# A gated attention and MLP kernel: which x chunks are turned by TensorE, and the order of the first transfers on SP's queue

## The chip, the cores and the metric

The kernel runs on one core of a Trainium2 chip. The metric is device time in microseconds (us) of one execution; of several executions the median counts, and less is better. Besides, one execution is taken by the hardware profiler; all durations of single instructions come from that one.

## What is computed

The input x has 2048 rows (tokens) of 640 bf16 numbers. Two blocks read it, and a gate per row mixes them:

```
g = sigmoid((x * gate_w).sum(-1))
out = g * A(x) + (1 - g) * B(x)

A: q, k, v = split(x @ wqkv)                 # 32 heads of 20
   phi(t) = where(t > 0, t + 1, exp(t)) + 1e-6
   kv = sum_s phi(k) v ;  z = sum_s phi(k)
   o  = phi(q) kv / (phi(q) z + 1e-6) ;  A = o @ wo
B: h  = gelu(layernorm(x) @ w1), its four quarters shifted by 1, -1, 2, -2 rows
   x1 = x + h @ w2 ;  B = x1 + gelu(layernorm(x1) @ w3) @ w4
```

For the change only the start of A matters: k = x @ wk, where wk is the middle third of wqkv, and phi(k).

## The kernel before

TensorE (PE) contracts over the 128 partitions, so x @ wk needs x transposed. The rows are tiled into 16 chunks of 128 (NCH), the 640 columns into 5 slabs of 128 (DC). `x_sb` holds x as it lies in memory, `xT` holds it transposed, `wkg` holds wk in five slabs with two more columns (the gate's weights and ones), hence 642 columns.

`k_mm(c, p, dc)` (L258) adds slab dc of chunk c into PSUM buffer p with two matmuls, of 512 and 130 columns. When a chunk has its five slabs, `k_post` (L263) applies phi: an exponential on ScalarE (ACT, L252), then two operations on VectorE (DVE, L255 and L256), the second of which writes phi(k) to `pk`; then it releases the PSUM buffer. There are four such buffers, handed out by `alloc` and `release` in the order of a list, `free`. From chunk 5 on, `g_unit(0, c)` is woven in: two matmuls of `x_sb` chunk c with `pk` chunk c (L269), which accumulate x^T phi(k) and hold one more PSUM buffer.

The order of the instructions on each engine is written by hand (`manual_schedule`). DMAs are issued from two queues: SP's (`sp`) and ACT's (`aq`). A queue issues in the order of the program and stands still while the next DMA waits for a semaphore. In the head it goes like this:

- ACT's queue: the gate's weights (L162), then slabs 0, 1 and 2 of wk (L166, `load_wk`). SP's queue: x chunks 0, 1 and 2 into `x_sb` (L156, `load_x`), then slabs 3 and 4 of wk in one DMA (L173).
- PE runs warm-up matmuls (L317) on zeros, then turns chunk 0 by five transposes against the identity matrix into PSUM (`x_tr`, L326), which DVE and ACT copy to `xT` (`x_cp`, L330 and L331). Then a small transpose of the gate's weights (L336), another warm-up, and chunk 1 the same way.
- A memset of DVE (L342) writes one element of `xT` in the place of chunk 3. The first transposing DMA (`load_xT`, L159), of chunk 3, overwrites that element and so waits for the memset. Behind it on SP stand all the other DMAs of `late_loads` (L285): transposing DMAs of the chunks up to 15, the x chunks from 3 on in between, then wq (L301), w1, wv, wo and w2. POOL's copies (L312) are part of it too.
- PE does slab 0 of chunks 0 and 1, turns chunk 2, and finishes the slabs of the three chunks in a woven order. Chunks 3 to 15 follow in a loop, chunk by chunk, then the q stage (L404), which reads wq.

After that follow the q stage, the layernorm and w1 stage, w2, w3 and w4, each a long run of matmuls; the change does not touch them.

Of the kernel before, what the change touches and what calls it, by code (L numbers as in the profile page):

```python
# [16 lines left out]
def kernel(  # L17
# [13 lines left out]
    nc = tc.nc  # L31
    P = 128
# [3 lines left out]
    NCH = S // P  # L36
# [28 lines left out]
    xT = RXT[:].rearrange("p (j s) -> p j s", j=DC)  # L65
# [71 lines left out]
    free = [0, 1, 2, 3]  # L137

    def alloc():
        return free.pop(0)  # L140
# [11 lines left out]
    sp, aq = nc.sync, nc.scalar  # L152
    xv = x2.rearrange("(c p) d -> p c d", p=P)

    def load_x(c0, c1):
        sp.dma_start(x_sb[:, c0:c1, :], xv[:, c0:c1, :])  # L156

    def load_xT(c0, c1):
        sp.dma_start_transpose(xT[:, :, c0 * P:c1 * P], x2[c0 * P:c1 * P, :])  # L159
# [5 lines left out]
    def load_wk(q, dc):  # L165
        q.dma_start(wkg[:, dc, 0:D], A_wqkv[dc * P:(dc + 1) * P, D:2 * D])  # L166

    for dc in range(3):
        load_wk(aq, dc)
    load_x(0, 1)  # L170
    load_x(1, 2)
    load_x(2, 3)
    sp.dma_start(wkg[:, 3:5, 0:D], A_wqkv[3 * P:5 * P, D:2 * D].rearrange("(j p) d -> p j d", p=P))  # L173


# [65 lines left out]
    def pop(q, n=1):  # L241
        for _ in range(n):
            if q:
                q.pop(0)()
# [13 lines left out]
    def k_mm(c, p, dc):  # L258
        for (n0, n1) in ((0, 512), (512, KW)):
            mm(PP[p][:, n0:n1], lhsT=xT[:, dc, c * P:(c + 1) * P], rhs=wkg[:, dc, n0:n1],  # L260
               start=(dc == 0), stop=(dc == DC - 1))

    def k_post(c, p):  # L263
        phi(pk[:, c, :], PP[p][:, 0:D], D, (ym[:, c, :], PP[p][:, D:D + 2]))
        release(p)
# [12 lines left out]
    def g_unit(i, c):  # L278
        if c == 0:
            gp[0] = alloc()  # L280
        g_step(i, c, gp[0])
        if c == NCH - 1:
            g_post(i, gp[0])

    def late_loads():  # L285
        load_xT(3, 4)
        load_xT(4, 5)
        load_xT(5, 6)
        load_xT(6, 7)
        load_x(3, 4)  # L290
        load_xT(7, 8)
        load_x(4, 6)
        load_xT(8, 10)
        load_x(6, 9)
        load_xT(10, 11)
        load_xT(11, 13)
        load_x(9, 12)
        load_xT(13, 16)
        load_x(12, 16)
        rows = lambda w, a, b: w[:, a:b].rearrange("(j p) d -> p j d", p=P)  # L300
        sp.dma_start(wq, rows(A_wqkv, 0, D))  # L301
        sp.dma_start(w1, rows(B_w1, 0, D))
        sp.dma_start(wv, rows(A_wqkv, 2 * D, 3 * D))
        sp.dma_start(wo6[0:GW, 0:5, :], A_wo[0:5 * GW, :].rearrange("(g r) d -> r g d", r=GW))
        sp.dma_start(wo6[0:GW, 5, :], A_wo[G5:D, :])
        sp.dma_start(w2[:, 0:4, :], B_w2.rearrange("(g c) d -> c g d", c=CG)[0:P])
        for g in range(4):
            sp.dma_start(w2[32 * g:32 * (g + 1), 4, :], B_w2[CG * g + P:CG * (g + 1), :])
        w1g = w1.rearrange("p k (g c) -> p k g c", c=CG)
        w1x4 = w1x.rearrange("p k (g c) -> p k g c", g=4)  # L310
        for g in range(4):
            nc.gpsimd.tensor_copy(w1x4[:, :, g, :], w1g[:, :, g, P:CG])  # L312


    def warm_up(n):
        for _ in range(n):
            mm(PP[1][:, 512:1024], lhsT=warm[:, 0:1].to_broadcast([P, P]), rhs=warm[:, 0:1].to_broadcast([P, 512]),  # L317
               start=True, stop=True)

    warm_up(5)  # L320

    def x_tr(c, a, b):
        ta, tb = PP[a][:, 0:512].bitcast(BF16), PP[b][:, 0:512].bitcast(BF16)
        for dc in range(DC):
            t, k = (ta, dc) if dc < 3 else (tb, dc - 3)
            nc.tensor.transpose(t[:, k * P:(k + 1) * P], x_sb[:, c, dc * P:(dc + 1) * P], ident[:])  # L326

    def x_cp(c, a, b):
        ta, tb = PP[a][:, 0:512].bitcast(BF16), PP[b][:, 0:512].bitcast(BF16)
        nc.vector.tensor_copy(xT[:, 0:3, c * P:(c + 1) * P], ta[:, 0:3 * P].rearrange("p (j s) -> p j s", j=3))  # L330
        act(xT[:, 3:5, c * P:(c + 1) * P], tb[:, 0:2 * P].rearrange("p (j s) -> p j s", j=2), ACT.Copy)  # L331
# [3 lines left out]
    tg = PP[0][:, 512:1024].bitcast(BF16)  # L335
    nc.tensor.transpose(tg[:, 0:DC], g5[0:DC, :], ident[0:DC, 0:DC])  # L336
    warm_up(1)
    for dc in range(DC):
        nc.vector.tensor_copy(wkg[:, dc, D:D + 1], tg[:, dc:dc + 1])
    x_tr(1, 1, 0)  # L340
    x_cp(1, 1, 0)
    nc.vector.memset(xT[:, 0, 3 * P:3 * P + 1], 0.0)  # L342
    late_loads()
    hp = (3, 2, 1)
    del free[1:]
    k_mm(0, 3, 0)
    k_mm(1, 2, 0)
    x_tr(2, 1, 0)
    x_cp(2, 1, 0)
    k_mm(0, 3, 1)  # L350
    k_mm(1, 2, 1)
    k_mm(2, 1, 0)
    k_mm(2, 1, 1)
    for c in range(3):
        k_mm(c, hp[c], 2)
    for c in range(3):
        for dc in (3, 4):
            k_mm(c, hp[c], dc)
        k_post(c, hp[c])


    for c in range(3, NCH):
        p = alloc()
        for dc in range(DC):
            k_mm(c, p, dc)
        k_post(c, p)
        for k in {5: (0, 1), 6: (2, 3), 7: (4,)}.get(c, (c - 3,) if c > 5 else ()):
            g_unit(0, k)
        if c % 2 == 0:
            pop(ln1_s)  # L370


# [359 lines left out]
```

## Time and profile before

| what | us |
|---|---|
| median of 5 runs | 265.08 (264.41 to 265.44) |
| the profiled execution's own time | 264.86 |
| its span in the profile | 263.1 |
| PE busy | 257.4 |
| DVE, ACT, POOL busy | 126.6, 109.7, 36.3 |
| five transposes of one chunk on PE (L326), in the chain | 0.53 |
| issue of one transposing DMA on SP (L159), chunks 3 to 7 | 1.22 to 1.29 |
| first transposing DMA issued at | 5.36 |
| first matmul of the k stage at | 4.91 |
| first matmul of the q stage at | 31.7 |

How to read it: times count from the start of the span. PE is the matmul side of TensorE, PEld its weight loads, which overlap with the matmuls. L12 is line 12 of the kernel. A group's line names the engine, the operation, the tile that it writes and those that it reads, the shapes and the count. In the timeline the first number is the start, the second the length. A bracket or "<-" behind an idle time names what ended it. SPq and ACTq are the parts of SP and ACT that issue DMAs; "to landing" is from the issue of a DMA to its last semaphore update. Tiles appear by the names of their memory: RXT is `xT`, RXH holds `x_sb`, RA holds `wkg` and `wq`, RPK is `pk`, and pp is PSUM.

### The profile page before, as it was taken

How to read it: one execution, taken by the hardware profiler on the slowest of the kernel's cores; microseconds unless marked ns; L12 is line 12 of the kernel's file. 1: busy time of each engine (PE TensorE's matmuls, PEld its weight loads, DVE VectorE, ACT ScalarE, POOL GpSimd, SP SyncE). 2: the span in 40 equal slices, each digit the busy share in tenths (PEclk: the TensorE clock that was granted, in tenths of full speed). 3: DMA queues.
4: the chain of work that ended last, by engine and by line, in shares of the span. 5: the costliest groups of instructions: out<-in, count | busy, mean ns of one | idle time of the engine just before them, and what ended most of it. 6: DMA issues, size and time to landing. Idle time of an engine off the chain costs nothing.

```text
span 263.1 us, 4153 instructions
## 1 busy us (share of the span) xinstructions
PE 257.4 (98%) x1634; PEld 136.3 (52%) x1666; DVE 126.6 (48%) x227; ACT 109.7 (42%) x163; POOL 36.3 (14%) x120
## 2 busy tenths in 40 slices
PE   8999999999999999999999999999999999999995
PEld 4555555555564545554444455555544445555552
DVE  1487658988995257999920023422310002334133
ACT  3466654554454761335977432202034445202200
POOL 7000053030200001446870000000000000000000
PEclk9999999999999999999999999999999999999999
DMA  6699998442242059992542000200200000010011
GB/s 200 131 214 211 351 268 177 93 52 50 50 52 50 13 139 404 325 164 50 108 96 50 0 2 0 75 27 0 77 25 0 0 2 0 0 51 26 25 52 50
DMA packets 42372, 24.07 MB, mean 91 GB/s; under 512 B 31137, under 2 KB 41585, under 8 KB 42353
## 3 DMA queue, kind: packets, MB, share of 16 engines
q1 hardware_dynamic: 41767, 23.28, 36.9%
q10 hardware_dynamic: 586, 0.53, 0.6%
q8 instruction: 13, 0.21, 0.4%
q14 instruction: 6, 0.05, 0.0%
HBM read 12.98 MB, written 3.44 MB: 62 GB/s over the span
## 4 chain that ended last, share of the span: by engine, by line
PE 98%; issue 1%; DVE 0%
PE pp L643 21%; PE pp L587 20%; PE pp L260 9%; PE pp L617 8%; PE pp L269 8%; PE pp L404 8%; PE pp L437 8%; PE pp L572 8%; PE pp L596 2%; PE pp L317 1%; PE pp L649 1%; PE pp L606 1%; PE pp L326 1%; PE pp L457 1%; PE pp L469 1%
## 5 line engine op out<-in xcount | busy, mean ns | idle before, releaser
L643 PE MATMUL pp<-RB,RXH 128*128 128x128 bf16 (+1 forms) x407 | 57.7, 297 | 0.7 <-issue 0.3
L587 PE MATMUL pp<-lnxT,RA 128*128 128x512 bf16 x236 | 51.9, 379 | 0.2
L643 PEld LDWEIGHTS <-RXH 128*128 128x128 bf16 x416 | 31.8, 98 | 24.5
L587 PEld LDWEIGHTS <-RA 128*128 128x128 bf16 x240 | 23.4, 98 | 28.1
L589 ACT ACTIVATE RXH<-pp 128x1024 bf16<-128x1024 f32 x24 | 24.3, 1021 | 30.5 <-PE pp L587 30.5
L252 ACT ACTIVATE eb<-pp 128x640 bf16<-128x640 f32 (+1 forms) x26 | 21.4, 829 | 25.2 <-PE pp L404 16.3
L620 ACT ACTIVATE RXH<-pp,g_all 128x640 f32<-128x640 f32 x16 | 12.7, 794 | 45.4 <-PE pp L617 45.4
L622 DVE SCALAR_TENSOR_TENSOR RPK<-RPK,omg,RXH 128x640 f32<-128x640 f32 x8 | 7.1, 884 | 41.5 <-ACT RXH L620 41.5
L269 PE MATMUL pp<-RPK,RXH 128*128 128x512 bf16 (+1 forms) x158 | 25.1, 298 | 0.1
L260 PE MATMUL pp<-RA,RXT 128*128 128x130 bf16 (+1 forms) x156 | 24.3, 303 | 0.2
L404 PE MATMUL pp<-RXT,RA 128*128 128x512 bf16 x98 | 23.1, 379 | 0.1
L617 PE MATMUL pp<-Mp,pqT 128*128 128x128 bf16 (+1 forms) x158 | 22.9, 298 | 0.1
L622 DVE SCALAR_TENSOR_TENSOR RXT<-RXT,omg,RXH 128x640 f32<-128x640 f32 x8 | 7.1, 884 | 31.9 <-ACT RXH L620 31.9
L572 PE MATMUL pp<-w,RXH 128*128 128x128 bf16 (+1 forms) x157 | 21.7, 297 | 0.2
L437 PE MATMUL pp<-lnxT,RB 128*128 128x512 bf16 x76 | 18.1, 379 | 0.2
L269 PEld LDWEIGHTS <-RXH 128*128 128x128 bf16 x160 | 12.7, 98 | 10.4
L260 PEld LDWEIGHTS <-RXT 128*128 128x128 bf16 x160 | 12.7, 100 | 9.6 <-DVE RXT L342 0.3
L617 PEld LDWEIGHTS <-pqT 128*128 128x128 bf16 x160 | 12.3, 98 | 9.9 <-issue 0.4
L572 PEld LDWEIGHTS <-RXH 128*128 128x128 bf16 x160 | 12.3, 98 | 9.5
L404 PEld LDWEIGHTS <-RA 128*128 128x128 bf16 x100 | 11.1, 117 | 9.2 <-DMA RA<-in_A_wqkv_dram 0.3
L255 DVE TENSOR_SCALAR eb<-eb 128x640 bf16<-128x640 bf16 (+1 forms) x26 | 9.5, 364 | 11.7 <-ACT eb L252 11.7
L256 DVE SCALAR_TENSOR_TENSOR RPK<-pp,eb 128x640 bf16<-128x640 f32 x16 | 13.2, 824 | 2.1
(112 smaller groups left out, 238.8 us busy)
## 6 DMA issues: line engine op xcount, KB each, us to landing
out_dram<-RXH SPq DMA_DIRECT2D x15, 160.0 KB, 1.8
RA<-in_B_w_dram SPq DMA_DIRECT2D x5, 432.0 KB, 6.8
RA<-in_A_wqkv_dram SPq DMA_DIRECT2D x2, 800.0 KB, 6.7
RB<-in_B_w_dram SPq DMA_DIRECT2D x1, 1120.0 KB, 9.1
RXH<-in_A_x_dram SPq DMA_DIRECT2D x2, 480.0 KB, 4.4
RB<-in_B_w_dram SPq DMA_DIRECT2D x1, 960.0 KB, 10.4
RB<-in_B_w_dram SPq DMA_DIRECT2D x1, 800.0 KB, 8.4
Mp<-Mscr SPq DMA_DIRECT2D x1, 800.0 KB, 4.3
```

Source lines behind the costliest of these rows:

```text
L252: act(e[:, 0:n], src, ACT.Exp)
L256: nc.vector.scalar_tensor_tensor(dst, src, 0.0, e[:, 0:n], op0=ALU.max, op1=ALU.add)
L260: mm(PP[p][:, n0:n1], lhsT=xT[:, dc, c * P:(c + 1) * P], rhs=wkg[:, dc, n0:n1], start=(dc == 0), stop=(dc == DC - 1))
L269: mm(PP[p][:, n0:n1], lhsT=x_sb[:, c, i * P:(i + 1) * P], rhs=pk[:, c, n0:n1], start=(c == 0), stop=(c == NCH - 1))
L404: mm(PP[p][:, tt * 512:(tt + 1) * 512], lhsT=wqp[:, dc, j], rhs=xT[:, dc, t0:t0 + 512], start=(dc == 0), stop=(dc == DC - 1))
L437: mm(PP[p][:, tt * 512:(tt + 1) * 512], lhsT=lh, rhs=lnxT[:, dc, t0:t0 + 512], start=(dc == 0), stop=(dc == DC - 1))
L572: mm(PP[p][:, n0:n1], lhsT=hsT[:, fc, 2 + c * P:2 + (c + 1) * P], rhs=w2[:, fc, n0:n1], start=(fc == 0), stop=(fc == DC - 1))
L587: mm(PP[p][:, k * 512:(k + 1) * 512], lhsT=w3[:, dc, (fc + k) * P:(fc + k + 1) * P], rhs=lnxT[:, dc, t * 512:(t + 1) * 512], start=(dc == ...
L589: act(h2T[:, t % 2, fc:fc + 2, :], PP[p][:].rearrange("p (k s) -> p k s", k=2), ACT.Gelu_apprx_tanh)
L617: mm(PP[p][:, n0:n1], lhsT=pqT[:, j, c * P:(c + 1) * P], rhs=Mp[:, j, n0:n1], start=(j == 0), stop=(j == DC - 1))
L622: nc.vector.scalar_tensor_tensor(x1(c), x1(c), omg[:, c:c + 1], ga, op0=ALU.mult, op1=ALU.add)
L643: mm(PP[ps[m]][:, n0:n1], lhsT=h2T[:, k, fc, i * P:(i + 1) * P], rhs=w4[:, fc, n0:n1], start=(m < 2 and fc == 0), stop=(m >= 2 and fc == N ...
```

## The change

Slab 2 of wk goes from ACT's queue to SP's, to the place where x chunk 2 was loaded. Chunk 2 is no longer turned by PE: a transposing DMA brings it, the first of five (chunks 2 to 6) that open `late_loads`. The memset that held back the first of these is gone, and `late_loads` is called ahead of PE's warm-up, so that on SP it stands directly behind slabs 3 and 4. Chunk 2 in its natural layout is loaded together with chunk 3, after the five. On PE chunks 0 and 1 go through slabs 0, 1 and 2 in turn, then each through slabs 3 and 4; chunk 2 has become the first of the loop. The first four PSUM buffers are given out as before (3, 2, 1, 0).

```diff
-    for dc in range(3):
-        load_wk(aq, dc)
+    load_wk(aq, 0)
+    load_wk(aq, 1)
     load_x(0, 1)
     load_x(1, 2)
-    load_x(2, 3)
+    load_wk(sp, 2)
     sp.dma_start(wkg[:, 3:5, 0:D], A_wqkv[3 * P:5 * P, D:2 * D].rearrange("(j p) d -> p j d", p=P))
...
     def late_loads():
-        load_xT(3, 4)
-        load_xT(4, 5)
-        load_xT(5, 6)
-        load_xT(6, 7)
-        load_x(3, 4)
+        for c in range(2, 7):
+            load_xT(c, c + 1)
+        load_x(2, 4)
         load_xT(7, 8)
...
+    late_loads()
     def warm_up(n):
...
     x_tr(1, 1, 0)
     x_cp(1, 1, 0)
-    nc.vector.memset(xT[:, 0, 3 * P:3 * P + 1], 0.0)
-    late_loads()
-    hp = (3, 2, 1)
-    del free[1:]
-    k_mm(0, 3, 0)
-    k_mm(1, 2, 0)
-    x_tr(2, 1, 0)
-    x_cp(2, 1, 0)
-    k_mm(0, 3, 1)
-    k_mm(1, 2, 1)
-    k_mm(2, 1, 0)
-    k_mm(2, 1, 1)
-    for c in range(3):
-        k_mm(c, hp[c], 2)
-    for c in range(3):
+    hp = (3, 2)
+    free[:] = [1, 0]
+    for dc in range(3):
+        for c in range(2):
+            k_mm(c, hp[c], dc)
+    for c in range(2):
         for dc in (3, 4):
             k_mm(c, hp[c], dc)
         k_post(c, hp[c])
...
-    for c in range(3, NCH):
+    for c in range(2, NCH):
...
-        if c % 2 == 0:
+        if c > 3 and c % 2 == 0:
             pop(ln1_s)
```

## The prediction

> **What bounds the kernel now.** I read the page's busy shares and its chain first. TensorE (PE) is busy for 98% of the span and makes up 98% of the chain that ended last, so only time taken from PE, or PE's idle time, moves the end.
>
> ```profile
> PE 257.4 (98%) x1634; PEld 136.3 (52%) x1666; DVE 126.6 (48%) x227; ACT 109.7 (42%) x163; POOL 36.3 (14%) x120
> ...
> PE 98%; issue 1%; DVE 0%
> ```
>
> Next the chain of waits over the first 30 us, which prices PE's pieces (start, length, what).
>
> ```profile
> 5.12 1.07 PE pp L260 x4
> 6.19 0.53 PE pp L326 x5
> 6.73 3.35 PE pp L260 x24
> ...
> 18.66 1.36 PE pp L260 x10
> ```
>
> The third chunk's five transposes (L326) are 0.53 us of it. Two matmuls of a k_mm (512 and 130 columns) cost 0.535 us before them (1.07/2), but 0.272 us later (1.36/5): PE starts at half speed. Mean durations of the 128x512 form by window say the same: 632 ns in 4.8 to 6.0 us, 379 ns in 8 to 14 us. The single records put the change near 6.8 us: matmuls of 512 columns start 0.427 us apart until then, 0.215 us after. The PEclk row (9 throughout) doesn't show it.
>
> ```profile
> L260 PE MATMUL pp<-RA,RXT 128*128 128x512 bf16 x2 | 1.2, 632 | 0.0
> ...
> L260 PE MATMUL pp<-RA,RXT 128*128 128x512 bf16 x22 | 6.2, 379 | 0.0
> ```
>
> Then who waits in 6 to 33 us, and what SP's queue waits for:
>
> ```profile
> PEld L404 <- DMA RA<-in_A_wqkv_dram: 0.3, 1, 0.3
> PEld L260 <- DMA RXT<-in_A_x_dram: 0.2, 1, 0.2
> ...
> SPq L159 <- DVE RXT L342: 2.7, 1, 2.7
> ```
>
> PE hardly waits for DMA, but two transfers have no slack: the transposition of chunks 13 to 15 (landed 26.66 us, asked for at 26.6) and wq (issued at 24.92, 6.7 us to landing, 31.67; PE is free at 31.61). The SP queue stood 2.7 us behind L342's memset before it issued the first transposition at 5.36. Third, the timeline around 14.9 us:
>
> ```profile
> 14.08 0.82 DVE L256 SCALAR_TENSOR_TENSOR RPK<-pp,eb 128x640 bf16<-128x640 f32 x1
> 14.22 0.43 PEld L269 LDWEIGHTS <-RXH 128*128 128x128 bf16 x4
> 14.27 0.71 PE L269 MATMUL pp<-RPK,RXH 128*128 128x512 bf16 x4
> ...
> 14.76 1.38 PEld L260 LDWEIGHTS <-RXT 128*128 128x128 bf16 x10
> ...
> 14.96 1.52 PE L260 MATMUL pp<-RA,RXT 128*128 128x512 bf16 x10
> ```
>
> Chunk 6 takes the PSUM buffer that VectorE (DVE) frees at 14.90; its matmul starts at 14.96, 0.14 us later than its four predecessors require. I compared all PE starts after 6.86 us with their columns: real holes are only this one (0.14), chunk 13 (0.03) and wq (0.10); gaps of 0.215 us are missing records. After 32 us there are only small fixed gaps, none on a DMA. What the head saves therefore reaches the end.
>
> **The change, part by part.**
>
> *Transposes of chunk 2 removed.* By the row it is 0.53 us. [...] If speed comes at the same moment, the 0.53 us is filled with k_mm work at half speed that would have cost 0.27 at full speed: gain 0.27. Had it ended with the work, 0.53. I take 0.27, since everything before 5.99 us stays as it is; 0.53 is the upper end. The two copies (DVE 0.36, ACT 0.38 us) and L342's memset (0.06) lie beside PE and are worth nothing: the second k_mm waits for x_cp(1), done at 5.31, not for the memset.
>
> *wk slab 2 from ACT to SP, in the place of x chunk 2.* x chunk 2 landed 3.5 us after its issue at 1.72, so slab 2 lands near 5.2 instead of 6.7. ACT issues one DMA fewer (0.45 us), ahead of its table load; nothing on PE waits for that. The new k_mm order (both chunks, slab by slab) asks for slab 2 at 6.9 us and for slabs 3 and 4 at 7.45. Those landed at 6.9 before (issue 2.18, 4.7 us), and now have 160 KB less beside them: 6.4 to 6.9. No wait; 0.5 us of cover.
>
> *Transpositions directly behind the loads on SP, without the gate.* Issues take 1.31 us each from 2.65 us: chunk 2 at 2.65, chunks 3 to 6 at 3.96, 5.27, 6.58, 7.89; x chunks 2 and 3 at 9.2; chunk 7 at 9.85 instead of 11.26. What follows on SP, up to wq, goes 1.4 us earlier: 2.7 won, one more transposition paid. SP holds only DMA issues here; POOL's four copies (L312) keep their place among POOL's instructions. When does PE ask? Two k_mm done at 5.99; 0.775 us at half speed is 1.45 k_mm; the other 6.55 at 0.272 take until 8.55. Chunk 2 is asked for at 8.55, chunks 3, 4, 5 at 9.9, 11.3, 12.6; two g_units (0.27 each) later chunk 6 at 14.5.
>
> When does chunk 2 land? Lower end 3.2 us from issue, the shortest in the window: 5.9. Upper end: chunk 10 behind a 480 KB load took 6.2 us (15.07 to its semaphore at 21.27): 8.85, a wait of 0.3. The nearest row is chunks 8 and 9, directly behind a 320 KB load as here, 4.8 us: 7.45. I take 7.5, with 1.1 us of cover. Chunks 3 to 6 land about 3.3 us after their issue, as before, or 0.8 us after one another: latest 8.3, 9.1, 9.9, 11.2. All earlier than asked for. If the cover is gone, each microsecond of lateness costs one.
>
> [...]
>
> *x chunk 2 later.* Its first reader is g_unit(0, 2) at about 15.9 us. Issued at 9.2, 4.1 us (as the 320 KB x load at 12.53), it lands near 13.3. Free.
>
> *Post-processing starts earlier.* Chunk 0's k_mm end at 8.0 instead of 9.1, as it no longer waits for chunk 2's. DVE's chain (1.19 us each: 0.32 + 0.82 and gaps) frees chunk 3's buffer at 13.8 instead of 14.9, and chunk 6 asks at 14.5: the hole of 0.14 goes. The PSUM buffers of chunks 3 to 7 are the same as before.
>
> *The two DMA waits.* PE now asks for chunks 13 to 15 at about 26.2 and for wq at 31.17. They land 1.0 to 1.4 us earlier (25.3 to 25.7; 30.3 to 30.7), the 1.0 because x chunk 2 now travels in this queue. Both fit: 0.13 gained, with 0.5 us of cover. Next late is then nothing: PE is full.
>
> Sum: 0.27 + 0.14 + 0.03 + 0.10 = 0.54 us. Span 263.1 to 262.6; the profiled execution took 264.86 (1.76 around the span), so 264.3. The median of the runs is 265.08, 0.22 above that one; minus 0.54 is 264.54. Some of these 0.22 should be waits on the transfers without slack, which the change covers too; I count 0.14: **264.4**.
>
> **Rivals.** What a measurement of this kernel can tell from no change is about 0.2%, 0.53 us.
>
> (1) *The wait moves to wq* (0.19). DMA throughput, not issue, sets when wq lands: queue traffic from 13 us on is dense (a share of 1.11 of the engines' time in 14.2 to 31.7 us), and more transposition bytes stand in line. Each 0.1 us that wq lands after 31.17 takes 0.1 us of the gain; if it lands at 31.67, all is lost. Against it: gaps in that traffic, and 1.4 us of earlier issue. Middle: 264.8, within 264.55 to 265.2.
>
> (2) *Slower: the third chunk's transposition is late* (0.15). It is queued behind the slabs, and its packets can stand still until the last DMA engine has finished the load ahead (behind x chunks 4 and 5 they stood for up to 1.0 us near 15.6); PE idles ahead of chunk 2. It decides from a landing at 9.1 us (the 0.54 is used up); from 9.6 it is measurably slower. Landing at 10.0 means a wait of 1.45: 266.0. For it: transposition behind a plain load took up to 6.2 us. Against it: that gives only 8.85.
>
> (3) *The gate is not gone* (0.03): transpositions still issue near 5.4 us, since something else holds them; chunk 2 lands at 8.7 or later, the next ones 1.31 apart: slightly slower, 265.7.
>
> (4) *Full speed comes earlier* (0.13): with fewer holes and more matmuls, or the runs' jitter on the two transfers counts for more: 263.4 to 264.1, middle 263.9.
>
> **How the numbers follow.** The forecast has 0.50, and its own range is 264.1 to 264.8, 0.37 of it under 264.55. Faster: 0.37 + 0.13 + 0.02 of (1) = 0.52. Same: 0.13 + 0.17 of (1) = 0.30. Slower: (2) and (3), 0.18. The range 263.7 to 265.4 leaves out the lower part of (4), about 0.06, and most of (2) and (3), about 0.13.
>
> **What would show it.** Right: five transposition issues from about 2.65 us; no L326 after 5 us; chunk 2's first k_mm near 8.55 us; chunk 2 landing before 8.5 us; PEld L260 and L404 without a DMA wait; wq's first matmul near 31.17 instead of 31.72. Wrong: "PEld L260 <- DMA RXT" of some tenths near 8.5 us, a wait for RA at 7.4, wq still at 31.7, or the step of PE's speed at another time than 6.8 us.

## The result, and the profile after

The changed kernel takes 264.22 us (median of 38 runs, 263.51 to 265.26), the kernel before 265.18 (75 runs beside it). The ratio is 0.9963, with a 95% interval of 0.9953 to 0.9974: 0.7 to 1.2 us faster, 0.98 in the middle. The forecast was 264.4, from 265.08: 0.54 us by its sum and 0.14 more by a guess. The direction and the place were right; one term, the waits on two transfers, was too small.

The profiled execution took 264.26 us, its span is 262.5 instead of 263.1. SP's timeline of after (start, length, engine, line, what) has no gap between slabs 3 and 4 and the first transpositions:

```profile
1.72 0.42 SPq L166 DMA_DIRECT2D RA<-in_A_wqkv_dram  x1
2.18 0.43 SPq L173 DMA_DIRECT2D RA<-in_A_wqkv_dram  x1
2.66 6.57 SPq L159 DMA_TRANSPOSE RXT<-in_A_x_dram  x5
9.28 0.58 SPq L156 DMA_DIRECT2D RXH<-in_A_x_dram  x1
```

In the chain of after one group of five transposes stands ahead of the k matmuls, and no second one among them:

```profile
4.56 0.53 PE pp L325 x5
5.09 5.23 PE pp L260 x32
10.31 0.05 issue
10.37 3.76 PE pp L260 x27
14.13 0.54 PE pp L269 x4
14.67 1.36 PE pp L260 x10
```

The 0.05 is one missing record, not a wait: PEld has a weight load at 10.15 whose matmul is not in the trace (L260 has 156 matmuls and 160 weight loads on the page). Chunk 2's transposition landed 4.3 us after its issue, at 6.95, and was asked for at 8.52. Chunk 6's ten matmuls follow the four of L269 without the hole of 0.14. Who waits in 6 to 33 us, in after:

```profile
ACT eb L252 <- PE pp L260: 10.0, 14, 2.7
DVE eb L255 <- ACT eb L252: 7.7, 11, 3.6
PEld L260 <- issue: 0.5, 2, 0.3
```

The two waits of PE on a DMA, for RXT and for RA, are gone. The q stage (L394 in this kernel) starts at 31.12 instead of 31.71:

```profile
30.85 0.43 PE L269 MATMUL pp<-RPK,RXH 128*128 128x512 bf16 x2
31.12 2.10 PE L394 MATMUL pp<-RXT,RA 128*128 128x512 bf16 x9
```

All of the change lies ahead of that point: from there to the end of the span it is 231.3 to 231.4 us in all 14 profiles of this study. So in what follows a profile is read by two numbers: when PE changes from half speed to full speed (single records of 512 columns start 0.427 us apart before it and 0.215 after; the moment itself is from the trace's records of the granted clock), and when the q stage starts. Beside them stand the holes, the idle gaps of PE ahead of the q stage.

### The profile page after: what moved, and what is told of

Its sections match the earlier page's. It is cut to its first block, busy times and chain, and to the rows that moved or that the text cites. A ratio compares the mean times of both kernels' runs of the same rounds, so it can differ in the third digit from the quotient of the medians.

```text
span 262.5 us, 4138 instructions
## 1 busy us (share of the span) xinstructions
PE 256.7 (98%) x1629; PEld 135.9 (52%) x1661; DVE 126.3 (48%) x225; ACT 109.4 (42%) x162; POOL 36.3 (14%) x120
## 4 chain that ended last, share of the span: by engine, by line
PE 98%; issue 1%; DVE 0%
PE pp L633 21%; PE pp L577 20%; PE pp L260 9%; PE pp L607 8%; PE pp L269 8%; PE pp L427 8%; PE pp L562 8%; PE pp L394 8%; PE pp L586 2%; PE pp L316 1%; PE pp L639 1%; PE pp L596 1%; PE pp L447 1%; PE pp L459 1%; PE pp L473 0%
## 5 line engine op out<-in xcount | busy, mean ns | idle before, releaser
L269 PE MATMUL pp<-RPK,RXH 128*128 128x128 bf16 (+1 forms) x158 | 25.1, 298 | 0.1
L260 PE MATMUL pp<-RA,RXT 128*128 128x512 bf16 (+1 forms) x156 | 24.3, 305 | 0.2
L394 PE MATMUL pp<-RXT,RA 128*128 128x512 bf16 x98 | 23.1, 379 | 0.1
L269 PEld LDWEIGHTS <-RXH 128*128 128x128 bf16 x160 | 12.7, 98 | 10.4
L260 PEld LDWEIGHTS <-RXT 128*128 128x128 bf16 x160 | 12.8, 100 | 9.9 <-issue 0.7
L394 PEld LDWEIGHTS <-RA 128*128 128x128 bf16 x100 | 11.1, 117 | 9.1
```

The lines of the kernel that those rows point to most:

```text
L269: mm(PP[p][:, n0:n1], lhsT=x_sb[:, c, i * P:(i + 1) * P], rhs=pk[:, c, n0:n1], start=(c == 0), stop=(c == NCH - 1))
L394: mm(PP[p][:, tt * 512:(tt + 1) * 512], lhsT=wqp[:, dc, j], rhs=xT[:, dc, t0:t0 + 512], start=(dc == 0), stop=(dc == DC - 1))
```

## The experiments

There were twelve experiments, each with 7 to 12 timed runs beside runs of the kernel before. Eight were made for the forecast's own terms. Four (after again, the second run of two wq DMAs in after, and the last two below) were made for a theory that came out of those: that in most executions the landing of wq, and not PE, sets when the q stage starts. The ratios are formed with the runs beside each kernel, so a ratio and a difference of two medians can differ by some tenths of a microsecond.

| kernel | median us | ratio to before (95%) | full speed from, us | q stage from, us | holes ahead of it, us |
|---|---|---|---|---|---|
| before | 265.18 | | 6.76 | 31.71 | 0.14, 0.03, 0.13 |
| before again | 265.05 | 1.0001 (0.9976 to 1.0026) | 6.71 | 31.92 | 0.14, 0.10, 0.31 |
| before, early queue | 264.65 | 0.9978 (0.9960 to 0.9996) | 6.65 | 31.80 | 0.14 |
| before, two wq DMAs | 264.68 | 0.9975 (0.9956 to 0.9994) | 6.40 | 31.86 | 0.42, 0.14 |
| before, order only | 265.26 | 0.9989 (0.9971 to 1.0008) | 4.51 | 32.30 | 0.39, 0.88 |
| before, early and two DMAs | 264.19 | 0.9977 (0.9957 to 0.9997) | 3.89 | 30.81 | 0.18, 0.14 |
| after | 264.22 | 0.9963 (0.9953 to 0.9974) | 6.72 | 31.12 | none |
| after again | 264.04 | 0.9960 (0.9940 to 0.9980) | 6.55 | 31.03 | none |
| after, dummy transposes | 264.24 | 0.9966 (0.9949 to 0.9984) | 4.20 | 32.13 | 1.68 |
| after, gate back | 266.70 | 1.0063 (1.0041 to 1.0085) | 5.87 | 32.83 | 0.77, 0.82, 0.20, 0.16 |
| after, one warm-up | 265.18 | 1.0008 (0.9991 to 1.0026) | 9.07 | 32.26 | none |
| after, two wq DMAs | 263.78 | 0.9952 (0.9937 to 0.9968) | 5.64 | 30.56 | none |
| the same again | 263.97 | 0.9961 (0.9943 to 0.9978) | 3.70 | 30.93 | 0.11, 0.57 |
| the same, dummy transposes | 264.27 | 0.9970 (0.9955 to 0.9986) | 4.93 | 31.07 | none |

The holes are those between PE's starts from 6 us on and at full speed, in order of time, with what the columns need taken off; in the first two rows they lie at chunk 6, at chunk 13 and at the first q matmuls. "The same" is after with two wq DMAs.

**The kernel before, again.** No edit.

> The kernel before, unchanged, for a second profile and for the size of chance. The measured gain of the change was 0.98 us, 0.54 of it accounted for by one pair of profiles. Theory (the two transfers without slack, chunks 13 to 15 and wq, land later in some executions): the ratio is 1.000, but the holes before chunk 13 and before the first q matmul differ from 0.03 and 0.10 us, and wq lands at another time than 31.67, by some tenths. Rival (the rest of the gain is chance, or sits elsewhere): the same holes to 0.03 us.

The ratio is 1.0001, and the holes are others: 0.10 us ahead of chunk 13 and 0.31 around the first q matmuls, where the first profile had 0.03 and 0.13. The chain of this second profile says who is late (start, length, what):

```profile
24.96 6.91 DMA RA<-in_A_wqkv_dram
31.87 0.05 issue
31.92 1.27 PE pp L404 x5
```

wq landed at 31.87 instead of 31.67. PE's last g_unit began at 31.38 and needed 0.27, so PE was free 0.2 us before that. One profile is not enough to size a wait with no slack.

**Early queue alone.**

```diff
+    late_loads()
     def warm_up(n):
...
-    nc.vector.memset(xT[:, 0, 3 * P:3 * P + 1], 0.0)
-    late_loads()
```

> Before with one part of the change alone: no memset gate, and the late loads called ahead of the warm-up, so that chunk 3's transposition stands directly behind slabs 3 and 4 on SP. TensorE's work and order stay. Theory: all transfers up to wq come 2.7 us earlier, the two DMA holes go (0.13 in the profile), the hole of 0.14 at chunk 6 and the transposes of chunk 2 stay: 0.13 us faster by the profile of before, and up to 0.4 us in the runs if the lateness of the two transfers is what the median holds beyond the profile. Rival (the gate protects the head's loads, and lifting it costs): a wait for slab 3 near 8.4 us or for x chunk 2, 0.2 us or more slower.

0.48 us faster than the runs beside it (264.65 against 265.13), with the interval from 0.1 to 1.1. Both DMA holes are gone, as expected; in this execution wq landed at 29.12. The hole at chunk 6 is still there: the four matmuls of L269 need 0.54 us, and L260 starts 0.68 after them.

```profile
14.50 0.71 PE L269 MATMUL pp<-RPK,RXH 128*128 128x512 bf16 x4
15.18 1.52 PE L260 MATMUL pp<-RA,RXT 128*128 128x512 bf16 x10
```

There is no wait for slab 3. What after has beyond this kernel is PE's own part, the removed transposes and the hole at chunk 6 (and one more transposition on the queue): after is 0.43 us faster in the medians (264.22 against 264.65), and redrawing the runs (drawing each set again and again with repetition, 95%) gives 0.15 to 0.76. The forecast has 0.27 + 0.14 = 0.41 for it. The span of 263.2 in the profile of the early queue is no contradiction to its gain: one of the sixteen semaphore counts of x chunk 1 came 0.6 us after the others (4.90), and the first k matmul was 0.55 us later than in before. The kernel with the order alone, which keeps the gate, shows the same lateness (4.83), so it need not come from the early queue.

**wq in two DMAs, in before.**

```diff
-        sp.dma_start(wq, rows(A_wqkv, 0, D))
+        wqr = rows(A_wqkv, 0, D)
+        sp.dma_start(wq[:, 0:2, :], wqr[:, 0:2, :])
+        sp.dma_start(wq[:, 2:5, :], wqr[:, 2:5, :])
```

> Before, with wq loaded by two DMAs (slabs 0 and 1, then 2 to 4) instead of one, so that its first slabs land about 1 us earlier, and nothing else. Theory: the hole before the first q matmul goes (0.10 by the profile, 0.1 to 0.3 in the median); 264.9 to 265.1 against 265.2. Rival (wq's landing has no part in it): no change.

0.45 us faster (264.68 against 265.13), interval 0.15 to 1.2; wq's first two slabs landed at 30.0, and PE's holes at chunk 13 and at the q stage are gone. The 0.42 in its profile is a wait for slab 1 of wk, whose last two semaphore counts came late (6.90). The gain is more than expected. wq's landing alone is worth about as much in the median as the whole early queue, and about four times the hole of 0.10 in the first profile. Redrawing the runs for the difference of medians gives -0.06 to 1.03, so its size is loose.

**Order alone.**

```diff
-    k_mm(0, 3, 1)
-    k_mm(1, 2, 1)
-    k_mm(2, 1, 0)
-    k_mm(2, 1, 1)
-    for c in range(3):
-        k_mm(c, hp[c], 2)
+    for dc in (1, 2):
+        k_mm(0, 3, dc)
+        k_mm(1, 2, dc)
     for c in range(3):
-        for dc in (3, 4):
+        for dc in range(DC) if c == 2 else (3, 4):
             k_mm(c, hp[c], dc)
```

> Before with another order of the k matmuls alone: chunks 0 and 1 go through all their slabs first, chunk 2 comes last. Transposes, gate and queues stay. Theory (the terms do not add up: what PE saves ahead of wq is lost again as long as wq lands at 31.7): the hole of 0.14 at chunk 6 goes, and the hole before the first q matmul grows by as much, to about 0.25; no change in time. Rival (the terms are independent): 0.14 us faster.

No change in time, as expected, and the hole at chunk 6 is gone. The place of the lost time was not the expected one. The timeline of this kernel around chunk 8 (PE and PEld only):

```profile
18.06 0.43 PE L269 MATMUL pp<-RPK,RXH 128*128 128x512 bf16 x2
...
19.21 0.66 PEld L260 LDWEIGHTS <-RXT 128*128 128x128 bf16 x6 [1.05 <-DMA RXT<-in_A_x_dram]
19.21 0.93 PE L260 MATMUL pp<-RA,RXT 128*128 128x512 bf16 x5 [0.72 <-DMA RXT<-in_A_x_dram]
```

Here full speed came at 4.51 us, 2.2 us earlier than in before, which is worth 1.1 us to PE. It went into waits: 0.39 for slab 2 of wk (landed at 7.12) and 0.88 for the transposition of chunks 8 and 9 (landed at 19.17). What PE saves in the head is only kept as far as the transfers are early.

**Dummy transposes in after.** Five transposes of chunk 0 behind slab 0 of chunks 0 and 1; their result is not used.

```diff
         for c in range(2):
             k_mm(c, hp[c], dc)
+        if dc == 0:
+            x_tr(0, 1, 0)
```

> After, with five more transposes of chunk 0 on TensorE at the place where before turned chunk 2; their result is not used, and no copies follow. Theory (half speed ends at a moment, near 6.7 us, not with a number of matmuls): the transposes take 0.53 us at half speed, but the q stage starts only 0.27 us later than in the profile of after; time 0.27 us over after, about 264.5. Rival (they cost what their row shows): 0.53 us over after, about 264.75.

0.02 us over after in the medians, 0.08 by the ratios. That is neither price, and the interval (about 0.45 us each way by the ratio) holds 0.27 and reaches 0.53. What the removed transposes bring in after itself is not settled by it. Its profile is no help for the time: one semaphore count of slab 1 of wk came 1.8 us after the others (7.30), and PE stood 1.68 us for it. It does show the two prices of the same instructions. In it full speed came at 4.20, and the transposes, after that, started 0.056 us apart (mean 219 ns in the groups), against 0.107 (314 ns) in before:

```profile
L325 PE MATMUL pp<-ident,RXH 128*128 128x128 bf16 x5 | 0.4, 219 | 0.0
```

**The gate put back.**

```diff
-    late_loads()
     def warm_up(n):
...
     x_cp(1, 1, 0)
+    nc.vector.memset(xT[:, 0, 2 * P:2 * P + 1], 0.0)
+    late_loads()
```

> After, with the gate put back: a memset of one element in chunk 2's place behind the copies of chunk 1, and the late loads behind it, so that transpositions issue from about 5.3 us again, chunk 2 first. Theory: all transfers come 2.65 us later than in after; chunk 2 lands near 8.2 to 8.6 and hardly holds PE, chunks 3 to 5 land about when they are asked for (9.9, 11.2, 12.5), and wq lands near 33.6 instead of 31.0: a hole before the q stage of about 2 us, 1.5 to 2.5 us slower than after, some 265.8 to 266.7. Rival (the early queue is of no weight, the gain is the removed transposes): within 0.2 us of after.

2.5 us slower than after in the medians (1.0% by the two ratios), the upper end of what was expected. The place was not the expected one: the holes are at chunk 3 (0.77), chunk 7 (0.82), chunk 8 (0.20), and only 0.16 is left at the q stage, where wq landed at 32.79. PE's waits of this kernel in 6 to 34 us:

```profile
PEld L260 <- DMA RXT<-in_A_x_dram: 2.3, 3, 1.0
PE pp L260 <- DMA RXT<-in_A_x_dram: 1.3, 2, 0.7
...
PEld L395 <- DMA RA<-in_A_wqkv_dram: 0.3, 1, 0.3
```

Without the early queue, then, the removed transposes bring nothing: this kernel is slower than before, too (ratio 1.0063), since the transposition that replaces them stands ahead of all the others on a queue that starts late.

**wq in two DMAs, in after,** twice, with the same edit as in before.

> After, with wq loaded by two DMAs (slabs 0 and 1, then 2 to 4). In the profile of after wq landed at 31.03 and PE asked for it at about 31.1, a slack of 0.1 us only. Theory (the slack is used up in some executions): 0.1 to 0.2 us faster than after, and less spread. Rival (wq is no longer late): no change from after.

> After with wq loaded by two DMAs, again, on the chip of its neighbours. Theory (wq is what after waits for in most executions): 0.3 to 0.45 us faster than after here too, 263.8, without a hole before the q stage. Rival (the first 0.44 was chance, since that profile's half speed ended 1.1 us earlier): less than 0.15 us faster than after.

The first time 0.4 us faster than after, the second time 0.07 (263.97 against 264.04, on the same chip one after the other). All runs together, 263.89 (22) against 264.13 (50): 0.24, and redrawing the runs gives 0.03 to 0.47. The lower profile of the first (span 261.9) owes about 0.5 us to full speed at 5.64. It is the fastest of all kernels, but whether wq still costs after something stays open. The second profile shows what is next: full speed at 3.70, and a hole of 0.57 ahead of chunk 8:

```profile
17.00 0.43 PE L269 MATMUL pp<-RPK,RXH 128*128 128x512 bf16 x2
17.85 1.48 PE L260 MATMUL pp<-RA,RXT 128*128 128x512 bf16 x9 [0.41 <-DMA RXT<-in_A_x_dram]
```

**One warm-up instead of five.**

```diff
-    warm_up(5)
+    warm_up(1)
```

> After, with one warm-up matmul instead of five ahead of the first transpose; PE then waits idle for x chunk 0 until 3.2 us, as it would anyhow. Tells what ends the half speed. [...] Rival (it ends at a fixed time from the start): full speed near 6.7 us again, no change in time.

0.96 us slower than after. Full speed came at 9.07 instead of 6.72; half of the 2.35 us between is 1.17, and the q stage starts 1.13 later. Mean durations of this kernel in two windows, 7 to 8.9 us and 9.2 to 12 us (one matmul of the second still shows the old speed):

```profile
L260 PE MATMUL pp<-RA,RXT 128*128 128x512 bf16 x5 | 2.8, 632 | 0.0
...
L260 PE MATMUL pp<-RA,RXT 128*128 128x512 bf16 x12 | 3.6, 400 | 0.0
```

So the moment is not a fixed time from the start: with four warm-up matmuls fewer it came later than in any of the thirteen profiles with five (3.70 to 6.76).

**After, again.**

> After, unchanged, for a second profile and as the reference of its neighbours. New theory: in most executions what sets the start of the q stage is the landing of wq, not TensorE, in before and still in after; in the first profile of after TensorE was as late as wq, because its half speed ended late (6.7 us). Where half speed ends earlier, PE waits for wq: a hole of some tenths before the first q matmul. Time as before, 264.2. Rival: no hole, as in the first profile of after.

No hole, as in the first profile of after. But full speed came late here too (6.55), so this execution did not put the theory to its test: wq landed at 30.72, and PE asked for it at 31.03, 0.3 us later.

**Two wq DMAs and dummy transposes.** Both edits together.

> After with wq loaded by two DMAs, and with five more transposes of chunk 0 on TensorE where before turned chunk 2 (result unused, no copies). In after these cost 0.02 us in the median. Theory (there the wait for wq covered them): with wq early they cost their full-speed price, 0.27 us over the kernel with two wq DMAs, about 264.1. Rival (transposes at that place are free): no more than 0.1 us over it. Rival (they cost what their row shows): 0.53.

0.30 us over the kernel with two wq DMAs beside it; redrawing gives -0.04 to 0.55, which alone excludes neither price. All runs of the two kernels with dummy transposes against all of the two without them give 0.23 (0.0 to 0.38). That fits the price at full speed, 0.27, and not 0.53.

**Before with the early queue and two wq DMAs.**

> Before without the gate, with the late loads ahead of the warm-up, and with wq loaded by two DMAs: all transfers come early, TensorE still turns chunk 2. Theory: against after with two wq DMAs only PE's own work is left, the five transposes (0.27) and the hole at chunk 6 (0.14): 0.4 us slower than it, 264.2, about as fast as after as it is. Rival (what after has over before is the transposes): 0.2 us or more slower than after.

264.19, as expected: 0.22 us over its neighbour with two wq DMAs (0.30 over all runs of that kernel), and 0.15 over after beside it; by the ratios it is 0.42 and 0.45. From 7 us on only the hole at chunk 6 is left. The forecast says 0.41 for PE's own part; 0.2 to 0.4 is measured here, and redrawing the runs gives 0.0 to 0.8, which holds it but does not prove it. The step from the early queue alone to after (0.43, 0.15 to 0.76) is the better measure.

## Why the prediction was right, and where it was short

- *Transposes removed: 0.27, not 0.53.* Upheld by the two kernels with dummy transposes (0.23 together, 0.0 to 0.38). No run shows that the half speed ends at a moment and not with the work, which the 0.27 takes; it was the author's estimate. What the profiles show is full speed at 6.76 in before and at 6.72 in after, so the work behind it moved up by one k_mm at full speed. That these two moments agree, as the forecast assumed, is luck: over the profiles with five warm-ups they differ by up to 3.1 us.
- *The hole at chunk 6: 0.14.* Right: it stands in each profile of before that keeps the old order, with or without the early queue, and is gone in the new one.
- *Chunk 2 and the other transpositions have cover.* Right: landed at 6.95 (7.5 forecast), asked for at 8.52 (8.55). wk slabs 3 and 4 landed at 6.30 and were asked for at 7.43. None of the rivals (2) and (3) shows.
- *The two DMA waits: 0.13, and 0.14 for the runs.* This is the term that was mis-sized. They are 0.16 in one profile of before and 0.41 in the other; the early queue alone gave 0.48 in the median, and two wq DMAs alone 0.45. The forecast took the holes of one execution for the typical ones. In both profiles of before full speed came late (6.76 and 6.71); in order alone it came earlier (4.51), and PE asked sooner and waited 1.27 us. That this is what the median holds is argued from that one profile, not measured. With the second pair of profiles the sum is 0.27 + 0.14 + 0.41 = 0.82, and the q stage starts 0.89 us earlier (31.92 to 31.03); full speed 0.16 us earlier makes up the 0.07. The forecast's 0.14 for the runs was a guess with the right sign.
- *Transfers 1.0 to 1.4 us earlier.* Half right: in the first pair of profiles those of chunks 13 to 15 were 1.04 us earlier (26.65 to 25.61), wq 0.64 (31.67 to 31.03; 30.3 to 30.7 was forecast); in the second pair 1.28 and 1.16 (31.87 to 30.72). Rival (1), the wait that moves to wq, was nearer than its chance said: 0.1 us of slack in the first profile, 0.3 in the second.
- *A sum of independent terms.* Only as long as the transfers are early. Order alone saves 0.14 us of PE time and gains nothing; with the gate put back, the removed transposes gain nothing. The queue is what makes PE's own savings count.

What sets the moment of full speed, no run shows. The traces' clock records give the moment itself, and the one when the clock falls back to half after the last matmuls (262.76 us in before, 262.72 in after). The stretch between them is 256.00 us long in eight profiles, these two among them, and 259.41 in the other six. Two executions of one kernel had full speed from 5.64 and from 3.70 us (two wq DMAs in after), and of the 14 profiles only that of the kernel with one warm-up lies outside 3.70 to 6.76, at 9.07.

What stays open: how much of the median of before is a wait on wq, and whether after still waits for it (two wq DMAs in after brought 0.44 and 0.07).

## What to carry to other kernels

If the engine on the path is full, size a wait on a transfer without slack by several executions: the one on wq was 0.13 us in one profile of before and 0.31 in the other, and wq in two DMAs brought 0.45 in the median. Time saved in a head at half speed need not count by its row: five transposes, 0.53 us by the row of before, cost 0.23 (0.0 to 0.38) here. And make the transfers early first: an engine's savings are kept only up to the next landing, so look at when each landing is asked for after the saving, not only at who waits now.

## What the runs showed of the hardware

- When PE's half speed ends differed between executions: it was at 5.64 and 3.70 us in two profiles of one kernel (two wq DMAs in after), at 3.70 to 6.76 over thirteen profiles, and at 9.07 with one warm-up. The 3.1 us of spread are up to 1.5 us of time, an estimate from the 0.427 and 0.215 us between matmuls of 512 columns. The PEclk row of before, 9 throughout, shows none of it. Transposes on PE ran at both speeds, 0.107 us apart in before and 0.056 with the dummy transposes.
- One or two of the sixteen semaphore counts of a load came late in some profiles: one of x chunk 1 0.6 us after the others with the early queue alone, one of slab 1 of wk 1.8 us after them with the dummy transposes. PE stood 1.68 us for the latter.
- A transposition directly behind a 320 KB load of wk landed in 4.3 us (4.1 to 4.7 over six profiles; 6.0 where the slab itself was late), against 3.2 to 3.4 in before for chunks 3 to 7, behind the gate.
